# Strided sparse attention and a Mish MLP on one core: batch 0's strided keys over two DMA queues, and a new order of the steps in every block

## Chip, core and metric

The kernel runs on one core of a Trainium2 chip, in one launch. The metric is device time in microseconds (us). A core has five engines with their own instruction queues: PE (TensorE: matmuls, and transposes done as matmuls), ACT (ScalarE), DVE (VectorE), POOL (GpSimd) and SP (SyncE). DMAs are issued from SP, from ACT (both through the hardware queues) and from POOL (through the software queue). Here only POOL's loads change the type on the way, from float32 in device memory to bf16 in the core's memory. An engine executes its own instructions in order; engines wait for one another on semaphores.

## What is computed

Eight batches of attention with 8 heads over 576 tokens, head size 64. Heads 0 to 3 see the last 32 positions, heads 4 to 7 the positions with the same remainder modulo 32. The result, 4608 tokens by 512, goes through an MLP.

```python
mask_local = (rel >= 0) & (rel < 32)
mask_strided = (rel >= 0) & (pos[None, :] % 32 == pos[:, None] % 32)
attn = softmax(where(mask, q @ k.T / 8, -1e9)) @ v
x = attn.transpose(0, 2, 1, 3).reshape(4608, 512)
h = x @ w_in                       # 512 x 2048
g = h * tanh(log1p(exp(min(h, 20))))   # h itself above 20
out = g @ w_out                    # 2048 x 512
```

## The kernel before

**Attention.** A batch b is a class `Attn` with a strided half ("s", heads 4 to 7) and a local half ("l", heads 0 to 3), each cut in parts: s0, s1, s2 and l0, l1, l2. For batches 0 to 2 the loaded rows `ks`, `qs`, `kl`, `ql` are transposed on PE (step `T`, two halves each) into a PSUM bank and copied from there to `kTs`, `qTs`, `kTl`, `qTl` (step `t`, on ACT or DVE); from batch 3 on SP transposes them by DMA (step `D`). Then for each part: `q` (scores, PE), `e` (Exp, ACT), `k` (mask, DVE; in batch 0 a bias `b` added on PE takes its place), `v` (times v, PE), `r` (division by the sum, DVE). `sp` copies the strided v to the layout in use, `sh` copies the rows of the local v that two windows share. `X` and `Y` transpose the result on PE, with `xc` and `yc` as their copies to `xT`; later batches do it by DMA (`y`, `V`, `vc`). `xT` holds four batches, a ring.

**MLP.** It goes in 9 blocks of 512 tokens. Block 0 uses plain products (`p1`, `pm`, `p2`, `oc`) for half of its first layer and all of its second. Everything else uses a form with seven products on 2 x 2 sub-blocks instead of eight. A first-layer group g (four per block) has the PE steps `1:g` to `7:g`, four matmuls of 256 columns each, and between them the copies and sums `1c`, `5c` (ACT or DVE), `6c`, `7c` (DVE), then the Mish activations `E`, `H`, `Z` (ACT). `6` adds to the bank that `1c` has to have read; `7` and `3` follow `6c`; `4` follows `7c`. Two sets of three PSUM banks (SET/EE) alternate between groups. The second layer of block t-1 has the steps `m1` to `m7` (two halves of eight matmuls) and runs at the start of block t. Sums of weights (`sw` for w_in, `so` for w_out), of inputs (`x`) and of activations (`g`, `n`) are on DVE.

**Order.** Nothing is scheduled by a compiler. Strings of such words, run through `do` one by one, set the order on every engine at once: `IN` (block 0), `SECOND`, `THIRD`, `MAIN` (used for blocks 3 and 4), `M5`, `M6`, `P7`, `PLAIN`, `LAST`. `un` is a matmul whose result nobody reads; it stands only where PE waits for the first loads.

**Loads.** POOL issues all loads but one pair: `stage_ks` (L134) has SP load batch 0's strided k in float32, two heads at a time, into `hh[0]` and `hh[1]`, and `cast_ks` (L137) turns them into bf16 `ks`. Eight loads of the software queue can be under way; the ninth waits for the first to land. The weights come in four pieces each (`wi`, `wo`).

Line numbers: L121 is every matmul through `mm`, L201 and L207 the transposes of strided and local rows, L110 and L112 copies on ACT and DVE, L115 sums on DVE, L275 and L273 Exp, L318 and L320 the division, L306 times v, L350 `X`/`Y`, L684 `pm`, L444, L446 and L448 the Mish steps E, H and Z, L130, L132, L143, L150, L154, L156, L159, L172 and L175 the loads of POOL.

Of the kernel before, what the change touches and what calls it, by code (L numbers as in the profile page):

```python
# [19 lines left out]
SU = 80  # L20
# [25 lines left out]
def kernel(ctx, tc, q, k, v, moe_w_in, moe_w_out, out):  # L46
# [81 lines left out]
    def load_str(b, n, src):  # L128
        if b == 0:
            Po.dma_start(raw[n][0:SU], rows80(src, 4, 4))  # L130
        else:
            Po.dma_start(raw[n][0:PN], src[b, 4:8].rearrange("h (p j) d -> p h (j d)", j=CS))  # L132

    def stage_ks(hp):  # L134
        nc.sync.dma_start(hh[hp][0:SU], rows80(k, 4 + 2 * hp, 2))

    def cast_ks(hp, eng):  # L137
        cast(eng, ks[0:SU, 2 * hp:2 * hp + 2, :], hh[hp][0:SU])
# [32 lines left out]
    def load_w_in(f0, f1):  # L171
        Po.dma_start(w_in[:, :, f0:f1], moe_w_in.rearrange("(cc p) f -> p cc f", p=128)[:, :, f0:f1])  # L172
# [382 lines left out]
    with tc.manual_schedule():  # L555
        Sc.preload_act_table(AF.Exp)
        Sc.dma_start(consts[:], consts_h.ap())
        for hp in range(2):
            stage_ks(hp)
# [48 lines left out]
        def do(w, t):  # L608
            if w[0] == "^":
                w, t = w[1:], t + 1  # L610
# [16 lines left out]
            elif f == "kc":  # L627
                cast_ks(int(x[0]), eng)
            elif f == "wi":
                load_w_in(int(x[0]), int(x[1]))  # L630
# [84 lines left out]
        def go(plan, t=0):  # L715
# [3 lines left out]
        IN = (  # L719
# [23 lines left out]
        )  # L743
        SECOND = (
# [7 lines left out]
        )  # L752
        THIRD = (
# [10 lines left out]
        )  # L764
        MAIN = (
# [8 lines left out]
        )  # L774
        M5 = (
# [8 lines left out]
        )  # L784
        M6 = (
# [66 lines left out]
```

## Time and profile before

| | before |
|---|---|
| median of 3 runs | 286.04 us (285.47 to 286.15) |
| the profiled execution's own time | 286.13 us |
| its span, first to last instruction | 284.4 us |
| PE busy / weight loads (PEld) | 276.1 us (97%) / 226.4 us (80%) |
| DVE busy | 220.4 us (77%) |
| ACT busy | 193.1 us (68%) |
| POOL busy | 51.8 us (18%) |
| granted TensorE clock | 1.000 |
| chain that ended last | PE 90%, DMA 3%, ACT 3%, DVE 1%, issue 1% |

A row of the timeline gives start, length, engine, line, operation, what it writes and reads, the size, and how many are merged into the row; in brackets the idle time of the engine ahead of it and what ended it. A busy PE counts each matmul until its result is out, so two matmuls overlap, and a short pause between two does not show as idle: start-to-start times show it. The difference between the profiled time and the span, 286.13 - 284.4 = 1.7 us, lies around the first and the last instruction.

### The profile page before, as it was taken

To read this page: it belongs to the slowest core of one execution; us is meant where nothing else is said; L and a number is where in the kernel's file an instruction comes from. 1 tells how busy PE (TensorE), PEld (TensorE's weight loads), DVE (VectorE), ACT (ScalarE), POOL (GpSimd) and SP (SyncE) were. 2 spreads that over 40 slices of the span, in tenths; PEclk is the share of its full clock that TensorE was granted. 3 is DMA by queue.
4 is the path that set the end of the run, shared out by engine and by line. 5 is a ranking of instruction groups with operands and counts; after the bars stand their busy time and mean duration, and the time that the engine had idled before them with its cause. 6 is when DMAs were issued, how large, how long until landed. Compare 5 with 4: busy or idle time off the path is not lost.

```text
span 284.4 us, 7635 instructions
## 1 busy us (share of the span) xinstructions
PE 276.1 (97%) x3242; PEld 226.4 (80%) x3242; DVE 220.4 (77%) x376; ACT 193.1 (68%) x296; POOL 51.8 (18%) x65
## 2 busy tenths in 40 slices
PE   8889999999999999999999999999999999999994
PEld 2656845668988888988898888898888888888883
DVE  2588978899897897999798969885999656835753
ACT  2686884599867777669765986678879427525830
POOL 8423321350007005200350044002000000000000
PEclk9999999999999999999999999999999999999999
DMA  7999999999849988999799979998472030003003
GB/s 157 191 206 204 205 189 199 103 222 167 148 90 93 131 154 150 205 145 170 208 143 126 179 204 160 121 168 189 97 190 48 2 120 28 2 3 148 2 0 148
DMA packets 103826, 38.50 MB, mean 135 GB/s; under 512 B 85384, under 2 KB 99112, under 8 KB 103792
## 3 DMA queue, kind: packets, MB, share of 16 engines
q0 software_dynamic: 61296, 18.62, 66.7%
q1 hardware_dynamic: 42208, 19.14, 28.3%
q8 instruction: 25, 0.41, 0.6%
q10 hardware_dynamic: 288, 0.25, 0.4%
q14 instruction: 9, 0.07, 0.1%
HBM read 38.03 MB, written 9.44 MB: 167 GB/s over the span
## 4 chain that ended last, share of the span: by engine, by line
PE 90%; DMA 3%; ACT 3%; DVE 1%; issue 1%; POOL 0%; ACTq 0%; DVEq 0%; POOLq 0%
PE set L121 57%; PE ee L121 21%; PE at L306 5%; PE at L121 4%; DMA kl<-in_k_dram 3%; PE at L350 1%; PE ee L207 1%; PE ee L350 1%; ACT osb L110 1%; DVE ee L115 1%; PE set L306 0%; ACT kTl L110 0%; ACT gT L684 0%; ACT Ps L273 0%; DVE x_s L320 0%
## 5 line engine op out<-in xcount | busy, mean ns | idle before, releaser
L121 PEld LDWEIGHTS <-wis 128*128 128x128 bf16 x578 | 55.7, 98 | 11.6 <-issue 2.9
L121 PEld LDWEIGHTS <-gs 128*128 128x128 bf16 x512 | 48.9, 98 | 6.3
L121 PEld LDWEIGHTS <-gT 128*128 128x128 bf16 x448 | 42.1, 98 | 9.4
L121 PEld LDWEIGHTS <-w_in 128*128 128x128 bf16 x436 | 41.1, 97 | 8.1 <-issue 1.0
L121 PE MATMUL set<-xT,w_in 128*128 128x256 bf16 (+1 forms) x296 | 45.8, 278 | 0.4 <-ACT gT L684 0.2
L121 PE MATMUL set<-w_out,gT 128*128 128x256 bf16 (+1 forms) x304 | 46.2, 295 | 0.0
L448 ACT ACTIVATE gT<-set 128x1024 bf16<-128x1024 f32 x35 | 35.9, 1025 | 12.6 <-PE set L121 12.3
L121 PE MATMUL set<-xs,wis 128*128 128x256 bf16 x280 | 42.0, 272 | 0.3 <-DVE ee L115 0.2
L110 ACT COPY set<-set 128x512 f32<-128x512 f32 x37 | 21.4, 577 | 18.8 <-PE set L121 18.3
L115 DVE TENSOR_TENSOR hh<-set,hh 128x512 f32<-128x512 f32 x35 | 24.0, 686 | 7.2 <-PE set L121 6.9
L115 DVE TENSOR_TENSOR ee<-set,hh 128x512 f32<-128x512 f32 x35 | 24.4, 697 | 5.7 <-PE set L121 4.0
L121 PE MATMUL set<-wos,gs 128*128 128x256 bf16 x224 | 27.8, 273 | 0.0
L446 ACT ACTIVATE gT<-hh 128x512 bf16<-128x512 f32 x35 | 21.7, 633 | 1.8 <-DVE hh L115 1.6
L115 DVE TENSOR_TENSOR gs<-gT,gs 128x2048 bf16<-128x2048 bf16 x16 | 19.5, 1219 | 3.3 <-issue 1.0
L673 POOL COPY hold<-xT 1x2 bf16<-1x2 bf16 x6 | 2.3, 381 | 105.4 <-DMA xT<-x_l 105.4
L444 ACT ACTIVATE gT<-ee 128x512 bf16<-128x512 f32 x35 | 20.0, 596 | 2.0 <-PE ee L121 2.0
L121 PE MATMUL ee<-xs,wis 128*128 128x256 bf16 x140 | 21.0, 273 | 0.0
L121 PE MATMUL set<-xs,w_in 128*128 128x256 bf16 x140 | 21.0, 272 | 0.0
L121 PE MATMUL ee<-xT,wis 128*128 128x256 bf16 x140 | 21.0, 273 | 0.0
L115 DVE TENSOR_TENSOR gs<-gT 128x2048 bf16<-128x2048 bf16 x16 | 19.5, 1217 | 0.0
L320 DVE TENSOR_TENSOR x_s<-at,rden 72x768 bf16<-72x768 f32 (+1 forms) x22 | 18.8, 856 | 0.8
L121 PE MATMUL ee<-wos,gT 128*128 128x256 bf16 x128 | 16.1, 273 | 0.0
(135 smaller groups left out, 439.7 us busy)
## 6 DMA issues: line engine op xcount, KB each, us to landing
out_dram<-osb SPq DMA_DIRECT2D x17, 512.0 KB, 3.3
ql<-in_q_dram POOLq DMA_DIRECT2D x8, 288.0 KB, 11.9
vl<-in_v_dram POOLq DMA_DIRECT2D x8, 288.0 KB, 12.0
w_in<-in_moe_w_in_dram POOLq DMA_DIRECT2D x4, 512.0 KB, 15.0
w_out<-in_moe_w_out_dram POOLq DMA_DIRECT2D x4, 512.0 KB, 16.9
ks<-in_k_dram POOLq DMA_DIRECT2D x7, 288.0 KB, 11.2
qs<-in_q_dram POOLq DMA_DIRECT2D x7, 288.0 KB, 10.4
vraw<-in_v_dram POOLq DMA_DIRECT2D x7, 288.0 KB, 9.4
```

The costliest lines, as they stand in the source:

```text
L110: Sc.copy(out_, in_)
L115: eng.tensor_tensor(out=out_, in0=a, in1=b, op=op)
L121: PE.matmul(o, lhsT=lhsT, rhs=rhs, start=start, stop=stop, skip_group_check=True)
L207: PE.transpose(tr[64 * e:64 * e + 64, PL * j:PL * j + PL], src[0:PL, 2 * hp + e, j, :], ident[0:PL, 0:PL],)
L306: PE.matmul(po[:, (n - n0) // per, (n - n0) % per, :], lhsT=pt[0:r, c0:c0 + 128], rhs=rhs, start=True, stop=True,)
L320: Dv.tensor_tensor(out=xo, in0=po[0:m, :, :, 0:D], in1=rd.unsqueeze(3).to_broadcast([m, nb, per, D]), op=ALU.mult,)
L350: PE.transpose(tr[:, n * j:n * j + n], x[0:n, u:u + 2, :].rearrange("p u d -> p (u d)"), ident[0:n, 0:n],)
L444: Sc.activation(o[:, 0:2, 256:512], two(E), AF.Mish)
L446: Sc.activation(o[:, 2:4, 256:512], two(h[:, 1, :]), AF.Mish)
L448: Sc.activation(o[:, :, 0:256].rearrange("p (b u) n -> p b u n", b=2), SET[z][:, 0:2, :].rearrange("p b (u n) -> p b u n", u=2), AF.Mish,)
L673: Po.tensor_copy(hold[0:1, 0:2], src)
```

## The change

Batch 0's strided k: SP loads the first two heads (`stage_ks`, `hh[0]`) as before; the other two come through the software queue straight into `ks` as bf16, as POOL's first load (`load_str` with h = 2). One cast is left, on ACT. The first quarter of w_in is loaded in two halves of its rows. All words are put in a new order, and every block has its own string in `PLANS`; `_` before a word means the block before, as `^` means the next. Blocks 8 and 9 have the words that PLAIN and LAST had, in the same order. What is computed stays the same; six more `un` matmuls are issued in front.

```diff
     def load_str(b, n, src):
         if b == 0:
-            Po.dma_start(raw[n][0:SU], rows80(src, 4, 4))
+            h = 2 if n == "ks" else 0
+            Po.dma_start(raw[n][0:SU, h:4], rows80(src, 4 + h, 4 - h))
...
-    def stage_ks(hp):
-        nc.sync.dma_start(hh[hp][0:SU], rows80(k, 4 + 2 * hp, 2))
-
-    def cast_ks(hp, eng):
-        cast(eng, ks[0:SU, 2 * hp:2 * hp + 2, :], hh[hp][0:SU])
+    def stage_ks():
+        nc.sync.dma_start(hh[0][0:SU], rows80(k, 4, 2))
+
+    def cast_ks(eng):
+        cast(eng, ks[0:SU, 0:2, :], hh[0][0:SU])
...
-    def load_w_in(f0, f1):
-        Po.dma_start(w_in[:, :, f0:f1], moe_w_in.rearrange("(cc p) f -> p cc f", p=128)[:, :, f0:f1])
+    def load_w_in(f0, f1, c0=0, c1=4):
+        Po.dma_start(w_in[:, c0:c1, f0:f1], moe_w_in.rearrange("(cc p) f -> p cc f", p=128)[:, c0:c1, f0:f1])
...
-        for hp in range(2):
-            stage_ks(hp)
+        stage_ks()
...
-            if w[0] == "^":
-                w, t = w[1:], t + 1
+            while w[0] in "^_":
+                w, t = w[1:], t + (1 if w[0] == "^" else -1)
...
-        IN = (
-            "ld:qs@0 ld:vs@0 kc:0:D kc:1:A un:1:a un:1:a un:1:a un:1:a un:1:a un:1:a un:1:a un:1:a clear:1 clear:0 b:s1:C@0 "
...
+        PLANS = (
+            (
+                "un:1:a ld:ks@0 un:1:a kc:A un:1:a un:1:a un:1:a un:1:a un:1:a ld:qs@0 un:1:a ld:vs@0 un:1:a un:1:a "
...
-        go(LAST, NBLK)
+        for t, plan in enumerate(PLANS):
+            go(plan, t)
```

Three places show how instructions move.

POOL at the very start, its first loads; `ks`, `qs`, `vraw`, `kl`, `ql`, `vl_78` belong to batch 0. Before:

```order
L130 DMA qs<-in_q_dram 80x4x512
L154 DMA vraw<-in_v_dram 80x4x512
L143 DMA kl<-in_k_dram 96x4x384
L143 DMA ql<-in_q_dram 96x4x384
L159 DMA vl_78<-in_v_dram 96x24x64
L172 DMA w_in<-in_moe_w_in_dram 128x4x512 x3
```

Now:

```order
L131 DMA ks<-in_k_dram 80x2x512
L131 DMA qs<-in_q_dram 80x4x512
L155 DMA vraw<-in_v_dram 80x4x512
L144 DMA kl<-in_k_dram 96x4x384
L144 DMA ql<-in_q_dram 96x4x384
L160 DMA vl_78<-in_v_dram 96x24x64
L173 DMA w_in<-in_moe_w_in_dram 128x2x512 x2
```

Half of k stands in front of everything on the software queue; the rest keeps its order, and the first quarter of w_in is two loads.

ACT in batch 0's attention (`Ps` and `Pl` are the Exp results of the strided and local parts, `ee_103` and `ee_104` the banks of the transposes). Before:

```order
L110 CAST ks<-hh_69 80x1024
L110 COPY kTs<-ee_103 128x8x72
L110 COPY qTs<-ee_104 128x8x72
L275 ACTIVATE Ps_86<-at 72x2x288
L275 ACTIVATE Ps_85<-set_102 72x2x432
L275 ACTIVATE Ps_84<-set_101 72x2x432
L110 COPY kTl<-ee_104 128x576
L110 COPY qTl<-ee_104 128x576
L110 COPY qTl<-ee_103 128x576
L275 ACTIVATE Pl_89<-at 128x2x384
```

Now:

```order
L110 CAST ks<-hh_68 80x1024
L110 COPY kTs<-ee_104 128x8x72
L110 COPY qTs<-ee_103 128x8x72
L110 COPY qTs<-ee_104 128x8x72
L276 ACTIVATE Ps_86<-at 72x2x288
L276 ACTIVATE Ps_85<-set_102 72x2x432
L276 ACTIVATE Ps_84<-set_101 72x2x432
L110 COPY kTl<-ee_103 128x576
L110 COPY qTl<-ee_104 128x576
L110 COPY qTl<-ee_103 128x576
L276 ACTIVATE Pl_89<-at 128x2x384
```

Both copies of the transposed q are now on ACT, ahead of the first Exp; DVE had one of them. On PE the transposes of `ql` moved ahead of two of the three `v` steps.

DVE where block 0 ends and block 1 begins (`wos` are the sums of w_out, `xs` those of the inputs, the copies those of batch 2's transposes, `set_101<-set_101` is `1c:0` of block 1). Before:

```order
L112 COPY kTs<-ee_104 128x8x72
L115 TENSOR_TENSOR xs<-xT 128x512
L115 TENSOR_TENSOR wos<-w_out 128x2048
L115 TENSOR_TENSOR wos<-wos,w_out 128x2048
L115 TENSOR_TENSOR wos<-w_out,wos 128x2048
L112 COPY qTl<-ee_104 128x576
L115 TENSOR_TENSOR xs<-xT,xs 128x512
L112 COPY qTl<-ee_103 128x576
L112 COPY vs<-vraw 72x32x64
L112 COPY vl_78<-vl_78 32x4x5x64
L112 COPY set_101<-set_101 128x512
```

Now:

```order
L115 TENSOR_TENSOR wos<-w_out 128x2048
L115 TENSOR_TENSOR xs<-xT 128x512
L112 COPY kTs<-ee_104 128x8x72
L115 TENSOR_TENSOR wos<-wos,w_out 128x2048
L115 TENSOR_TENSOR xs<-xT 128x512
L112 COPY qTs<-ee_103 128x8x72
L115 TENSOR_TENSOR wos<-w_out,wos 128x2048
L112 COPY kTl<-ee_103 128x576
L112 COPY qTl<-ee_104 128x576
L115 TENSOR_TENSOR xs<-xT,xs 128x512
L112 COPY qTl<-ee_103 128x576
L112 COPY set_101<-set_101 128x512
```

The big sums stand further ahead and apart from one another, one copy of `qTs` and one of `kTl` came over from ACT, and the two copies of v went behind `1c:0`.

More of the change, by code (lines that the diff above doesn't have):

```diff
@@ L627, in do @@
             elif f == "kc":
-                cast_ks(int(x[0]), eng)
+                cast_ks(eng)
             elif f == "wi":
-                load_w_in(int(x[0]), int(x[1]))
+                load_w_in(*(int(c) for c in x))
             elif f == "wo":
@@ L717, in go @@
                 do(w, t)
-        IN = (
[23 rows of a table removed]
-        )
-        SECOND = (
[7 rows of a table removed]
-        )
-        THIRD = (
[10 rows of a table removed]
-        )
-        MAIN = (
[8 rows of a table removed]
-        )
-        M5 = (
[8 rows of a table removed]
-        )
-        M6 = (
[7 rows of a table removed]
-        )
-        P7 = (
[5 rows of a table removed]
-        )
-        PLAIN = (
[4 rows of a table removed]
-        )
-        LAST = (
-            "m1c:D g:1 m5:0 m5:1 m5c:A g:2 m6:0 m6:1 g:3 m2:0 m6c:A m2:1 m7:0 m7:1 m7c z:b:D w:b:S m3:0 m3:1 m3c "
-            "st:1 m4:0 m4:1 z:1:A z:0:D w:0:S w:1:A "
-        )
-        go(IN)
-        go(SECOND, 1)
-        go(THIRD, 2)
-        for t in range(3, NBLK):
-            main = {5: M5, 6: M6}.get(t, MAIN)
-            if t + 1 < B:
-                go(" ".join(w for w in main.format(n1=t + 2, n2=t + 3).split() if int(w.partition("@")[2] or 0) < B), t)
-            else:
-                go(P7 if t + 1 == B else PLAIN, t)
-        go(LAST, NBLK)
+        PLANS = (
+            (
[23 rows of a table added]
+            ),
+            (
[7 rows of a table added]
+            ),
+            (
[10 rows of a table added]
+            ),
+            (
[8 rows of a table added]
+            ),
+            (
[8 rows of a table added]
+            ),
+            (
[8 rows of a table added]
+            ),
+            (
[7 rows of a table added]
+            ),
+            (
[5 rows of a table added]
+            ),
+            (
[4 rows of a table added]
+            ),
+            (
+                "m1c:D g:1 m5:0 m5:1 m5c:A g:2 m6:0 m6:1 g:3 m2:0 m6c:A m2:1 m7:0 m7:1 m7c z:b:D w:b:S m3:0 m3:1 m3c "
+                "st:1 m4:0 m4:1 z:1:A z:0:D w:0:S w:1:A "
+            ),
+        )
+        for t, plan in enumerate(PLANS):
+            go(plan, t)
 _INS = ['q', 'k', 'v', 'moe_w_in', 'moe_w_out']
```

150 rows, old and new, of tables (IN, M5, M6, MAIN) are left out of this document.

## The prediction

> **What bounds the kernel now.** I read the page first, then a table of stages, then the timeline in the stages where the table shows idle time. On the page PE has little left, and its clock is at full speed throughout:
>
> ```profile
> PE 276.1 (97%) x3242; PEld 226.4 (80%) x3242; DVE 220.4 (77%) x376; ACT 193.1 (68%) x296; POOL 51.8 (18%) x65
> PEclk9999999999999999999999999999999999999999
> ```
>
> The stages are cut where PE's work changes: waiting for k and q, batch 0's attention, the start of the MLP, block 0's rest, the hand-over to block 1, blocks 1 to 6, block 7, block 8 with the tail.
>
> ```profile
> core 0: us, PE busy (x) PEld busy (x) DVE busy (x) ACT busy (x) POOL busy (x), PEclk, DMA share, GB/s
> 0.00:8.60 8.60, 6.60 (x33) 2.34 (x33) 2.59 (x17) 2.86 (x3) 6.44 (x12) 1.00 0.86 166
> 8.60:19.30 10.70, 9.59 (x211) 6.70 (x211) 6.99 (x15) 8.18 (x14) 4.35 (x6) 1.00 1.47 197
> 19.30:28.00 8.70, 8.11 (x68) 5.22 (x66) 7.65 (x18) 5.59 (x8) 2.85 (x4) 1.00 1.25 204
> 28.00:57.00 29.00, 28.97 (x386) 18.27 (x384) 24.28 (x45) 19.94 (x32) 8.59 (x11) 1.00 1.33 174
> 57.00:64.00 7.00, 6.42 (x109) 4.74 (x109) 6.94 (x13) 7.00 (x14) 3.43 (x4) 1.00 1.63 223
> 64.00:225.00 161.00, 160.91 (x1950) 140.84 (x1949) 138.02 (x227) 122.52 (x188) 26.13 (x30) 1.00 1.12 145
> 225.00:256.00 31.00, 31.00 (x281) 27.18 (x279) 18.63 (x27) 14.52 (x23) 0.00 (x0) 1.00 0.09 36
> ```
>
> PE idles 0.59 us in 19.3 to 28, 0.58 us in 57 to 64, and 0.09 us in the 161 us after that. So a new order can win in the first 64 us, and by short pauses that busy time hides; in the 161 us it can only keep or lose. The first MLP product starts near 19.3; all before it is worth what batch 0's attention waits.
>
> **Part 1, the head (0 to 23.5).** These rows carry it:
>
> ```profile
> 0.74 0.90 SPq L135 DMA_DIRECT2D hh<-in_k_dram  x2
> 1.29 0.76 POOL L130 DMA_DIRECT2D qs<-in_q_dram  x1 [0.84 <-POOLq L836]
> 4.00:6.00 2.00, 2.00 (x7) 0.59 (x6) 0.54 (x1) 0.00 (x0) 2.00 (x4) 1.00 1.08 212
> hh<-in_k_dram SPq DMA_DIRECT2D x2, 320.0 KB, 5.1
> 8.64 0.57 PEld L201 LDWEIGHTS <-qs 72*128 72x128 bf16 x16 [0.41 <-DMA qs<-in_q_dram]
> 9.19 0.46 DVE L112 COPY qTs<-ee 128x576 bf16<-128x576 bf16 x1 [0.40 <-PE ee L201]
> 9.38 0.64 ACT L110 COPY qTs<-ee 128x576 bf16<-128x576 bf16 x1 [1.03 <-PE ee L201]
> 10.57 0.65 ACT L275 ACTIVATE Ps<-at 72x576 bf16<-72x576 f32 x1 [0.56 <-PE at L121]
> 11.54 0.45 PE L207 MATMUL ee<-consts_sb,kl 96*64 96x96 bf16 x12 [0.19 <-DMA kl<-in_k_dram]
> 14.23 1.18 ACT L110 COPY qTl<-ee 128x576 bf16<-128x576 bf16 x2 [0.85 <-PE ee L207]
> 17.00 0.87 ACT L273 ACTIVATE Pl<-ee 128x384 bf16<-128x384 f32 x2
> 19.20 0.95 DVE L320 TENSOR_TENSOR x_l<-at,rden 96x768 bf16<-96x768 f32 x1
> 20.44 0.41 DVE L115 TENSOR_TENSOR xs<-xT 128x512 bf16<-128x512 bf16 x1
> ```
>
> q's landing at 8.64 starts the chain. The GB/s count what is written. The change takes one 320 KB load off SP and puts 160 KB (80 x 1024 bf16) ahead of q on POOL's queue: 160 KB less in front of q, at 212 GB/s up to 0.77 us earlier. But q is issued one POOL instruction (0.76 us) later; if that is what starts its transfer, it lands up to 0.76 later. Between these ends I take -0.4, nearer the gain: q takes 7.3 us from issue to landing, far more than its issue, so it mostly queues for bandwidth.
>
> From landing to the first Exp it takes 10.57 - 8.64 = 1.93 us, with the two copies of q side by side. Now both are on ACT, one behind the other: the first at about 8.64 + 0.55 = 9.19, ends of 9.83 and 10.47 against 10.02 now, +0.45. Then ACT runs from 10.57 to 17.87 (17.00 + 0.87), and 0.85 us of that is idle ahead of the `ql` copies, since PE does all of v first. With the `ql` transposes ahead of two of the v steps most of it closes: -0.6, with 0 and -0.85 as bounds. Behind it on DVE come the divisions, and now a sum of x and one of w_in (0.41 each) ahead of the last copy to `xT`; the four matmuls that need no such copy cover most of it, +0.15. Of the cast that is gone (1.0 us, DVE) nothing counts: DVE waits there anyway. The local k (11.54, 0.19 idle) moves with q. Sum -0.4; ends -0.77 - 0.85 + 0.45 = -1.2 and 0.76 + 0.45 + 0.15 = +1.4. The split of w_in's first quarter costs one POOL issue behind all of batch 0's loads: nothing, as long as w_in is waited for nowhere. It landed by 17.95, ahead of 19.3:
>
> ```profile
> 17.95 0.76 POOL L175 DMA_DIRECT2D w_out<-in_moe_w_out_dram  x1 [1.95 <-DMA w_in<-in_moe_w_in_dram]
> ```
>
> The Trainium skill, "DMA: Bandwidth & Descriptors", section "Issuing engines are not separate DMA queues", says that DMAs from different engines run on the same 16 DMA engines and interleave, and that issuing from several saves only issue time. By that rule the split moves no landing, the head comes to +0.0 in place of -0.4, and the sum below to 285.5; no row here shows the two halves apart.
>
> **Part 2, the start of the MLP (19.3 to 28).**
>
> ```profile
> 23.48 0.60 PE L121 MATMUL set<-xT,w_in 128*128 128x256 bf16 x4 [0.25 <-ACT gT L684]
> 24.01 0.60 PE L121 MATMUL ee<-xs,wis 128*128 128x256 bf16 x4
> 24.17 0.57 ACT L110 COPY set<-set 128x512 f32<-128x512 f32 x1 [0.21 <-PE set L121]
> 24.79 0.60 PE L121 MATMUL set<-xT,w_in 128*128 128x256 bf16 x4 [0.18 <-ACT set L110]
> 26.09 0.42 PE L201 MATMUL at<-consts_sb,ks 72*128 72x72 bf16 x8
> 26.68 0.60 PE L121 MATMUL set<-xs,wis 128*128 128x256 bf16 x4 [0.16 <-DVE ee L115]
> 28.89 1.02 ACT L448 ACTIVATE gT<-set 128x1024 bf16<-128x1024 f32 x1
> ```
>
> A step of four matmuls takes 0.44 us start to start where nothing waits (256.26 to 256.69 in a row further down). `1:1` starts at 23.48, `5:1` at 24.01, `2:1` at 24.79: 0.34 us lost to `1c`. Ahead of `7:1` (26.68) eight transposes of about 0.31 us started at 26.09: 0.28 lost to `6c`. The first wait (Mish of block 0's bank) stays. Now `5:1` and `5:2` stand behind `1:1`, and both pairs of eight transposes ahead of `7:1`, so -0.62 at best. But `5:2` needs a DVE sum of w_in two places earlier than before, and the next user of the bank waits for the Mish step at 28.89 (1.02 us) as it does now, which may give it all back: 0 at worst. I take -0.35.
>
> **Part 3, the hand-over (57 to 64).** ACT is busy 7.00 of 7.00 and DVE 6.94. One copy of `qTs` and one of `kTl` (0.6 each) go from ACT to DVE ahead of this stage, and the three 1.22 us sums of w_out start earlier. What stays is the row of Exp steps, each of which frees a bank for the next scores and then for `1:1`:
>
> ```profile
> 58.29 0.92 ACT L275 ACTIVATE Ps<-at 72x864 bf16<-72x864 f32 x1
> 60.09 0.20 PE L121 MATMUL ee<-qTl,kTl 64*128 64x96 bf16 x1 [0.22 <-ACT Ps L273]
> ```
>
> The first Exp still stands behind the copy of block 0's output (`oc:0`), so I give it -0.15, between -0.58 (all idle gone) and +0.6 (one more Exp in front of `1c:1`).
>
> **Part 4, blocks 1 to 6.** `6` may start 0.87 us after the end of `1` (23.48 + 0.44 = 23.92 to 24.79) if ACT takes `1c` at once. The new strings put just two steps (0.88 us) between them in eleven groups, where the old ones had three or more; in return `7` now stands three steps behind `6`, not two. Where ACT happens to be inside another step, the wait is half of 0.57 to 1.02, some 0.4 us. For two such groups in eleven that is +0.8; for none 0, for six +2.4. The longer `6` to `7` brings back some 0.1 us each in three groups. I take +0.2, nearer to none since PE idles 0.09 us in all of the stage today with steps as tight as that.
>
> **Part 5, block 7.** Pauses that busy time hides, the first and the last of the stage:
>
> ```profile
> 232.52 0.60 PE L121 MATMUL ee<-xs,wis 128*128 128x256 bf16 x4
> 233.04 0.60 PE L121 MATMUL set<-xs,wis 128*128 128x256 bf16 x4
> 239.96 0.60 PE L121 MATMUL set<-xT,w_in 128*128 128x256 bf16 x4
> 240.39 0.60 PE L121 MATMUL set<-xs,wis 128*128 128x256 bf16 x4
> 240.97 0.60 PE L121 MATMUL set<-xs,w_in 128*128 128x256 bf16 x4
> 256.26 0.60 PE L121 MATMUL set<-xT,w_in 128*128 128x256 bf16 x4
> 256.69 0.60 PE L121 MATMUL set<-xs,wis 128*128 128x256 bf16 x4
> ```
>
> 239.96 to 240.39 is a step without a wait (0.43), 240.39 to 240.97 one with 0.14 behind it: two steps do not cover a 0.69 us sum on DVE with its hand-overs. The block has seven such places, from 0.08 (232.52 to 233.04) to 0.14; the new string has three steps in most. -0.3, between -0.6 and 0. Blocks 8 and 9 keep their order: 0.
>
> **Sum.** -0.4 - 0.35 - 0.15 + 0.2 - 0.3 = -1.0. Against the profiled execution's own 286.13 (span 284.4 and 1.7 around it) that is 285.1; the median of the runs, 286.04, lies 0.09 lower, so it is a gain of 0.33%. About 0.3% (0.86 us, 285.18) is what a measurement of this kernel can tell from no change. The likeliest case's own range is 284.3 to 286.0.
>
> **Rivals.** A, slower: ACT does not take `1c` at once in blocks 1 to 6. Six of eleven groups at 0.4 us are +2.4 in place of +0.2, so 287.3; it decides from about four groups on. For it: DVE is busy 138 of 161 us and ACT 122.5, so queues are rarely empty. Against: these engines run in order and the old strings leave 0.09 us idle at the same load. B, larger gain: q lands 0.77 earlier, and the moved sums free the hand-over of its whole 0.58 us: -0.8, -0.6 and -0.55 for parts 1 to 3 with 0 and -0.3 for 4 and 5: 283.9. For it, DVE full in 57 to 64; against, ACT full there too. C, no change: the software queue starts q one issue later, +0.7 in the head instead of -0.4, the rest as above: 286.2. For it the row at 1.29, where q is POOL's first load today.
>
> **How the numbers follow.** Forecast 0.50, A 0.27, B 0.12, C 0.11. Faster by over 0.3%: half of the forecast's case, a little over (0.28), all of B (0.12), some of the rest (0.03): 0.43. Within 0.3% (285.18 to 286.90): 0.20 of the forecast's, 0.08 of C, 0.01 of A: 0.29. Slower: 0.28. The range that leaves out 2 in 10 is 283.9 to 287.6: B's time at the low end, A with one group more at the high end.
>
> **What would show it.** Head: `qs` awaited near 8.2 (C: 9.3), no idle of ACT ahead of the `qTl` copies, `1:1` starting by 23.1. Start of the MLP: `2:1` and `7:1` without a wait. Hand-over: PE's idle at or below 0.5 us between the `ql` transposes and `6:1` of block 1. Blocks 1 to 6: PE idle below 0.5 us with no row of `6` behind an ACT copy; A is right if that idle exceeds 2 us. Wrong altogether: a DVE or PE step that waits for a load of batch 3 or later, which no part counts.

## The result: slower, and the profile after

| | before | changed |
|---|---|---|
| median | 286.04 us (285.47 to 286.15) | 302.85 us (4 runs, 299.72 to 308.04) |
| the profiled execution: time / span | 286.13 / 284.4 us | 308.04 / 306.2 us |
| ratio to the kernel before | | 1.055, 95% interval 1.047 to 1.064 |

The change costs some 16 us, far outside the predicted range. All ratios here leave out executions more than 1.5% longer than the shortest one of the same kernel, so a ratio can differ from that of two medians, and the profile after is of such an execution, the longest of its four. The first lines of the page after:

```profile
PE 281.7 (92%) x3248; PEld 228.6 (75%) x3248; DVE 220.3 (72%) x377; ACT 193.4 (63%) x294; POOL 51.7 (17%) x67
PEclk9999999999999999999989999999999997999999
PE 65%; DMA 10%; DVE 8%; issue 2%; ACT 1%; POOL 0%; DVEq 0%; ACTq 0%; POOLq 0%; SPq 0%
```

DVE and ACT are busy as long as before (220.4 and 193.1 us), so no work was added. PE fell from 97% to 92% of a longer span: it waits. On the chain that ended last its share fell from 90% to 65%, DMA rose from 3% to 10% and DVE from 1% to 8%. The stages of the prediction, now cut where about as many matmuls have been done (columns as there; the first two stages in one up to 19.3, the next two up to 58.8):

```profile
0.00:19.30 19.30, 16.94 (x250) 9.72 (x251) 8.28 (x29) 11.10 (x17) 11.99 (x20) 1.00 1.18 176
19.30:58.80 39.50, 35.85 (x445) 23.25 (x442) 30.79 (x61) 26.69 (x41) 11.08 (x14) 1.00 1.32 175
58.80:65.60 6.80, 6.43 (x117) 4.34 (x111) 6.42 (x11) 5.62 (x12) 3.08 (x3) 1.00 0.99 161
65.60:242.00 176.40, 164.41 (x1950) 141.53 (x1948) 138.85 (x228) 123.08 (x187) 25.52 (x31) 0.99 1.25 134
242.00:277.10 35.10, 32.89 (x281) 28.01 (x279) 20.68 (x31) 14.00 (x21) 0.00 (x0) 0.95 0.08 32
277.10:306.20 29.10, 25.17 (x227) 21.77 (x224) 15.27 (x20) 12.91 (x20) 0.00 (x0) 0.99 0.19 73
```

Against 19.3, 37.7, 7.0, 161.0, 31.0 and 28.4 us before: 0, +1.8, -0.2, +15.4, +4.1 and +0.7, together 21.8 us, more than the 16 since this execution is the longest. Blocks 1 to 6, where the prediction allowed 0.2 us, lose most. What PE waits for, by groups (engine, tile and line, what it waited for: us in all, times, longest):

```profile
PE set L121 <- DVE ee L115: 6.0, 12, 1.3
PE set L121 <- DVE osb L115: 2.4, 4, 0.8
PE at L307 <- DMA vl<-in_v_dram: 2.3, 1, 2.3
PE at L351 <- DVE xT L112: 1.6, 1, 1.6
PE at L208 <- DVE kTl L112: 1.2, 1, 1.2
```

None of these groups stands among the first six of before, where the largest of them measures:

```profile
PE set L121 <- DVE ee L115: 0.2, 1, 0.2
```

Line numbers from L129 on are one higher than before. Three places show three kinds of wait. The first, from the timeline of PE and DVE in block 2 (`6:1`, `2:0`, `4:0`, `2:1` and `7:1` on PE, the sum `6c:1` on DVE):

```profile
97.88 0.60 PE L121 MATMUL set<-xs,wis 128*128 128x256 bf16 x4
98.31 0.60 PE L121 MATMUL set<-xT,w_in 128*128 128x256 bf16 x4
98.75 0.60 PE L121 MATMUL set<-xs,w_in 128*128 128x256 bf16 x4
99.19 0.60 PE L121 MATMUL set<-xT,w_in 128*128 128x256 bf16 x4
...
99.89 0.70 DVE L115 TENSOR_TENSOR ee<-set,hh 128x512 f32<-128x512 f32 x1 [1.33 <-PE set L121]
...
100.65 0.60 PE L121 MATMUL set<-xs,wis 128*128 128x256 bf16 x4 [0.86 <-DVE ee L115]
```

`6:1` has ended by 98.48, and `6c:1` reads what it wrote; yet DVE, idle for 1.33 us, begins at 99.89, 0.1 us behind the end of `2:1` (99.79). `2:1` writes the other bank of the set. Then `7:1` waits for `6c:1`. The second kind, from the timeline of PE and ACT in block 1 (`X:0`, `X:1` and the copy `xc:0`):

```profile
73.21 0.42 PE L351 MATMUL at<-consts_sb,x_s 72*128 72x72 bf16 x8
...
73.94 0.65 ACT L110 COPY xT<-at 128x576 bf16<-128x576 bf16 x1
...
74.64 0.42 PE L351 MATMUL at<-consts_sb,x_s 72*128 72x72 bf16 x8 [1.01 <-ACT xT L110]
```

`X:1` writes a bank of its own, and still begins only when `xc:0` has read the other one (73.94 + 0.65 = 74.59). The third, the longest stall, from the timelines of POOL, PE and ACT:

```profile
145.02 2.40 POOL L160 DMA_DIRECT2D vl<-in_v_dram  x2
...
155.13 0.60 PE L121 MATMUL set<-xT,w_in 128*128 128x256 bf16 x4
158.06 0.22 PE L307 MATMUL at<-vl,Pl 128*128 128x65 bf16 x2 [2.33 <-DMA vl<-in_v_dram]
159.35 0.71 PE L307 MATMUL at<-vl,Pl 128*128 128x65 bf16 x10 [1.07 <-ACT vl L110]
159.87 1.90 PE L121 MATMUL set<-w_out,gs 128*128 128x256 bf16 x8
```

The local v of batch 5 lands 13 us after its issue. Behind the stall eight matmuls take 1.69 us from start to start (161.56 - 159.87 by the next row) where eight took 0.87.

The transposes that SP issues by DMA land later as well; issue to landing from 64 to 200 us, the kernel before first:

```profile
xT<-x_l SPq DMA_TRANSPOSE x10, 3.0
kTl<-kl SPq DMA_TRANSPOSE x5, 4.2
```

And the changed kernel:

```profile
xT<-x_l SPq DMA_TRANSPOSE x9, 7.2
kTl<-kl SPq DMA_TRANSPOSE x5, 9.7
```

So two theories. **Whole tiles**: the waits are kept per PSUM tile, not per bank. `SET[i]` and `AT` are each one tile of two banks, so two steps on different banks wait for each other, and which one waits is set by which is written first in the strings. The semaphore waits of the built programs, resolved to the steps, bear it out: in the kernel before no `2` waits for a `6c` and no `6c` for a `2`, since every `2` is written ahead of its `6`. The new strings put `2` behind `6` in 28 groups, and

```
14 groups: 6c:g waits for the last matmul of 2:g     (block 2: 6c:1 <- PE 2:1)
11 groups: 2:g waits for the sum 6c:g or 7c:g        (block 0: 2:2 <- DVE 6c:2)
 3 groups: neither
```

**Collision**: POOL's small copies (`hold`), by which the kernel before keeps the next loads back until the transposes of x have landed, wait for an older batch in the new strings and hold no load back: four of the six that run find their batch landed, and the two that wait, until 205.94 and 230.98 us, stand behind the last load (189.13). Loads and transposes then run together and both come late. The rivals kept from the prediction: ACT late for `1c` (no such wait is among the groups above), and the loads of batch 0.

### The profile page after: what moved, and what is told of

Read it like the earlier page. It is cut to its first block, busy times and chain, and to the rows that moved or that the text cites. A ratio compares the mean times of both kernels' runs of the same rounds, so it can differ in the third digit from the quotient of the medians.

```text
span 306.2 us, 7657 instructions
## 1 busy us (share of the span) xinstructions
PE 281.7 (92%) x3248; PEld 228.6 (75%) x3248; DVE 220.3 (72%) x377; ACT 193.4 (63%) x294; POOL 51.7 (17%) x67
## 4 chain that ended last, share of the span: by engine, by line
PE 65%; DMA 10%; DVE 8%; issue 2%; ACT 1%; POOL 0%; DVEq 0%; ACTq 0%; POOLq 0%; SPq 0%
PE set L121 41%; PE ee L121 15%; DMA vl<-in_v_dram 4%; PE at L307 3%; DMA kTs<-ks 3%; PE at L121 3%; DVE ee L115 3%; DMA xT<-x_l 3%; DVE gs L115 1%; DVE hh L115 1%; DVE osb L115 1%; PE ee L208 1%; DVE vl L112 0%; ACT vl L110 0%; PE at L351 0%
## 5 line engine op out<-in xcount | busy, mean ns | idle before, releaser
L121 PEld LDWEIGHTS <-wis 128*128 128x128 bf16 x584 | 56.9, 99 | 16.3 <-issue 6.5
L110 ACT COPY set<-set 128x512 f32<-128x512 f32 x33 | 18.9, 574 | 22.4 <-PE set L121 22.3
L110 ACT COPY osb<-set 128x1024 f32<-128x1024 f32 x9 | 9.1, 1013 | 12.3 <-PE set L121 12.3
L110 ACT COPY hh<-ee 128x512 f32<-128x512 f32 x22 | 12.9, 591 | 6.2 <-PE ee L121 6.2
```

What stands on the lines that cost most here:

```text
L110: Sc.copy(out_, in_)
L121: PE.matmul(o, lhsT=lhsT, rhs=rhs, start=start, stop=stop, skip_group_check=True)
```

## Experiments

Each ratio is to the kernel before, run beside it on the same chip. The changed kernel's is 1.055 (1.047 to 1.064); in us, a ratio is taken times 286.

**Step 2 ahead of 6 again (two_ahead).** In 28 groups, for instance in block 2:

```diff
- 5:1 E:0 6:1 5c:1:A 7c:0 k:s1:D@3 2:0 4:0 2:1 6c:1
+ 5:1 E:0 2:1 6:1 5c:1:A 7c:0 k:s1:D@3 4:0 6c:1
```

> The changed kernel with each step 2 of a first-layer group put back just ahead of step 6 of its group (28 groups of blocks 0 to 7); nothing else. Theory, whole tiles: SET is one tile of two banks, so 2 (which adds to the first bank) and the sum 6c (which reads the second) wait for each other although they share no byte; with 2 ahead of 6 no such wait is left. The 6.0 us in which PE waits for the sum 6c fall below 2, and the time falls by 4 to 8 us, to 294 to 299. Rival, ACT late for 1c: step 2 itself needs 1c, so the time stays within 1 us of the changed kernel's 302.9. Rival, late loads: within 1 us too.

297.31 us, ratio 1.041 (1.035 to 1.047). The group of the 6.0 us:

```profile
PE set L121 <- DVE ee L115: 1.7, 6, 0.4
```

As expected: some 4 us of the 16 (1.4%, between 0.3 and 2.5 by the two intervals) come back with nothing but the place of `2`. ACT's rival falls, since `2` too needs `1c`.

**The mirror: step 2 behind 6c in the kernel before (two_behind).** 16 words of the strings for blocks 3 to 7, for instance

```diff
- 2:2 6:2 ld:qs@{n2} 1:3 1c:3:A 6c:2 v:s2:A
+ 6:2 ld:qs@{n2} 1:3 1c:3:A 6c:2 2:2 v:s2:A
```

> The kernel before with one kind of step moved in blocks 3 to 6 (and block 7): each step 2 of a first-layer group from ahead of 6 to just behind the sum 6c in the strings, 16 moves over one to three places; its own input (1c) is long done there. Theory, whole tiles: 2 now waits for 6c, 0.5 to 2 us a group, and the time rises by 10 to 22 us, to 296 to 308. If banks counted singly: 2 waits for nothing and the time stays within 1 us of 286.2.

303.59 us, ratio 1.062 (1.059 to 1.065; two runs), with the head, the loads and all other words as before. The group that has 0.2 us in the kernel before is now the first:

```profile
PE set L121 <- DVE ee L115: 12.4, 14, 1.7
```

This step alone can cost what the whole change cost.

**Only the text (at_text).** Three copies of `AT` written one place later; for instance

```diff
- X:0:a xc:0:a:A ld:kl@3 X:1:A
+ X:0:a ld:kl@3 X:1:A xc:0:a:A
```

> The changed kernel with three copies written one place later in the strings (xc:0 behind X:1 in blocks 1 and 2, the second copy of batch 1's local k behind the transposes into the other bank). Every engine keeps exactly its order; only which of two steps on different banks of AT comes first in the program changes, and so which one waits. Theory, whole tiles: the stalls of 1.1 us at 73, 1.8 us at 110 and 1.2 us at 37 shrink, together by 2 to 4 us; the time falls to 299 to 301. Any theory that counts by banks or by the order on the engines: no change, within 0.5 us.

301.01 us, ratio 1.047 (1.044 to 1.050). No engine's order changes, and PE's wait of 1.01 us is gone, and with it the groups of 1.6 and 1.2 us in the list above (0.6 us for `qTs` stands in place of the last). The two transposes are one row, from the timeline of PE:

```profile
71.97 0.68 PE L351 MATMUL at<-consts_sb,x_s 72*128 72x72 bf16 x16
```

The interval still overlaps the changed kernel's, and the profiled execution (305.33 us) has other long waits for DVE, so the row carries this more than the time: a wait that comes and goes with the text, on two banks of one tile, is what whole tiles predict and a count by banks or engines excludes.

**Both edits (two_and_text).** 

> The changed kernel with both edits of the first runs: step 2 ahead of 6 in 28 groups, and the three copies of AT's banks written one place later. If both act on waits of their own, the gains add: 302.9 - 5.5 - 1.8 = 295.5, between 294 and 297. If the first stall only hands over to the next: no lower than 297.

297.54 us, ratio 1.041 (1.038 to 1.043). The gains don't add: nothing below the first edit alone. The timelines of SP, DVE and PE say where it went:

```profile
108.08 1.97 SPq L328 DMA_TRANSPOSE xT<-x_l  x1
...
116.64 0.42 DVE L115 TENSOR_TENSOR xs<-xT 128x512 bf16<-128x512 bf16 x1 [6.08 <-issue]
...
117.45 0.68 DVE L112 COPY o<-set 128x512 f32<-128x512 f32 x1
...
118.19 1.22 PE L121 MATMUL set<-wos,gs 128*128 128x256 bf16 x5 [3.85 <-DVE o L112]
```

DVE stood for 6.08 us ahead of a sum of x (`x:2` of block 3) that the built program lets wait for the two transposes of batch 3, and the copy `o`, which PE needs, stood behind it. Transposes land late here too:

```profile
xT<-x_l SPq DMA_TRANSPOSE x10, 6.9
kTl<-kl SPq DMA_TRANSPOSE x5, 12.6
```

**One load earlier (vl_early).**

```diff
- Z:0 _hold@2 H:0
+ Z:0 ld:vl@5 _hold@2 H:0
- m6:1 _ld:vl@5 e:s0:F
+ m6:1 e:s0:F
```

> The changed kernel with one load moved: the local v of batch 5 is issued in block 3, ahead of the wait of POOL for block 2's transposes, not in block 4 behind three other loads. Theory, late loads: the wait of 4.9 us of ACT and 2.3 us of PE for this load goes, and with it PE's 4.5 us of idle from 155 to 160, so the time falls by 3 to 6 us, to 297 to 300. Whole tiles alone: no change, within 1 us of 302.9.

302.85 us, ratio 1.056 (1.052 to 1.060): a miss. In the profiled execution (307.98 us) the wait for the local v is gone, and PE stands some 15 us earlier instead, behind DVE, which waits for the strided v:

```profile
142.40 0.69 DVE L112 COPY vs<-vraw 72x2048 bf16<-72x2048 bf16 x1 [4.37 <-DMA vraw<-in_v_dram]
...
143.75 1.01 PE L121 MATMUL set<-xT,w_in 128*128 128x256 bf16 x4 [4.32 <-DVE ee L115]
```

The stall is not tied to that one load: here another late load takes its place.

**No holding back, in the kernel before (no_hold).** The five `hold` words left out (six copies, since MAIN runs twice).

> The kernel before without the five small copies by which POOL waits for the transposes of x before it issues the next batch's loads; nothing else. Theory, transposes and loads collide: in the changed kernel these copies wait for an older batch and hold nothing back, the transposes of kTl take 9.7 us to land in place of 4.2 and those of xT 7.2 in place of 3.0. Without them the kernel before shows the same: xT above 4.5 us, and 0.5 to 4 us lost. Rival, the order of the strings alone: no change, within 0.5 us.

289.9 us median (10 runs, 285.94 to 292.68), ratio 1.007 (1.004 to 1.011). POOL in the kernel before, at the copy that waits for batch 2:

```profile
84.93 0.63 POOL L673 COPY hold<-xT 1x2 bf16<-1x2 bf16 x1 [23.04 <-DMA xT<-x_l]
```

POOL and PE in this run, profiled in an execution of 292.64 us:

```profile
79.34 0.71 POOL L132 DMA_DIRECT2D ks<-in_k_dram  x1 [17.73 <-DMA kTs<-ks]
...
92.87 1.04 PE L121 MATMUL set<-xT,w_in 128*128 128x256 bf16 x4 [3.91 <-DMA xT<-x_l]
```

Without it the loads of batch 4 start at 79.34, before that copy has even run, and PE then waits 3.91 us for transposes of x. These take 4.4 us in the middle, where above 4.5 was expected; the ratio is as expected, some 2 us. A wait of 3.91 us belongs to this long execution and not to the 2 us; no profile of a shorter one was taken. That the copies are worth something in the old order is shown, that the collision is what they prevent there is read off this one profile.

**Holding back, in the changed kernel (hold_back, hold_and_vl).** On top of both edits, the loads of batches 4 to 7 behind the transposes of x of two batches earlier. For batch 6 (of the strings, only the words that issue DMAs or run on POOL):

```diff
- y:1 _y:0 ld:vs@6 _ld:qs@6 _ld:ks@6 _ld:vl@5 ld:vl@6
+ y:1 _y:0 hold@4 ld:vs@6 _ld:qs@6 _ld:ks@6 _ld:vl@5 ld:vl@6
```

In the second run `ld:vl@5` also moved out of there to block 3, behind `ld:vs@5`.

> The run before with POOL's waits put back: the loads of batches 4, 5, 6 and 7 behind the transposes of x of batches 2, 3, 4 and 5, as the kernel before has them. Theory, collision: xT lands in 3 to 4.5 us, the stalls where DVE waits for xT near 91 and 150 shrink, 1 to 3 us below the run before. Rival: later loads make a wait of their own for k, q or v of batches 6 and 7, and the time rises.

> The run hold_back with one more edit: the local v of batch 5 issued in block 3, ahead of POOL's new wait for the transposes of batch 4, so that this load is not held back with the others. Theory, collision of loads and transposes: with the loads of the next batch kept off the transposes, and no load late for that, the one long stall of PE (3.6 to 4.4 us with the slower matmuls behind it) goes for good: 4 to 8 us below hold_back's 301.7 and 3 to 6 us below two_and_text's 297.5, to 291 to 295. Rival: the stall comes back at another load, and the time stays at 297 or above.

301.68 and 301.57 us, ratios 1.054 (1.048 to 1.060) and 1.055 (1.049 to 1.060): both slower than without, so the time follows the rival both times. xT lands in 3.2 us in both, as the theory has it, but other transfers are late in turn, and not the ones that the rivals named: in the first the local v of batch 5 (PE's waits),

```profile
PE at L307 <- DMA vl<-in_v_dram: 4.0, 1, 4.0
```

in the second the transposes of the strided x in block 6 (timeline of DVE):

```profile
205.18 1.34 DVE L112 COPY xT<-ks 128x576 bf16<-128x576 bf16 x2 [3.77 <-DMA ks<-x_s]
```

PE waits 4.2 us behind that copy. In the new strings, putting the old holds back moves the long stall on in both.

**A quarter of the bytes (light_two_and_text, light_after, light_load_alone).** Every instruction stays where it is; for instance in `load_str`:

```diff
+ n_h = 4 if b < 4 else 1
- ... src[b, 4:8] ...
+ ... src[b, 4:4 + n_h] ...
```

> The run two_and_text with the loads of batches 4 to 7 cut to one head of four (a quarter of the bytes; the other three heads then hold what an earlier batch left, so that part of the result is not computed). All instructions of all engines stay in number and order. Theory, collision: the loads no longer slow the transposes of xT, kTl and qTs, the one long stall (3.9 us with 2.4 us of slow matmuls behind it) is gone in every run: 289 to 292. Rival, the order of the strings on DVE is what stalls: 296 or more.

> The changed kernel with the loads of batches 4 to 7 cut to one head of four, in the same way. Theory: of the 302.9 us the part of the whole-tile waits stays and the part of the collisions goes: 302.9 less 5 to 8, so 295 to 298, and the spread of the runs (299.7 to 308.0) shrinks below 2 us. Rival: 301 or more.

> Control: the run load_alone with the same cut of the loads of batches 4 to 7. Theory: that order keeps loads and transposes apart already, so the time falls by no more than 1 us from 285.75.

292.14 us, ratio 1.021 (1.019 to 1.023), so 5.7 us (2.0%) less than with all bytes; 299.82, ratio 1.048 (1.045 to 1.051); and the control 285.12, ratio 0.997 (0.996 to 0.999), like load_alone below. In the first of the three:

```profile
xT<-x_l SPq DMA_TRANSPOSE x10, 3.1
kTl<-kl SPq DMA_TRANSPOSE x5, 4.8
```

This settles the collision where the tile waits are gone: with the same order on every engine and the bytes of four batches cut, xT lands in 3.1 us in place of 6.9 and the long stall is gone. The cut also makes the loads themselves land sooner (the local v in 3.0 us in place of 10.9); how much of the 5.7 us that is worth was not separated. In the changed kernel itself the same cut brings 2 us by the ratios, less than the 5 to 8 expected, and no more than that kernel's own interval; its spread shrinks from 8.3 to 2.0 us, as expected. So the two causes overlap: taking the tile waits away is worth 4 us with all bytes (1.055 to 1.041) and 7.8 with a quarter of them (1.048 to 1.021). That one wait covers another is the likely reason; no run shows it directly.

**The loads alone (load_alone).** The kernel before with `stage_ks`, `cast_ks` and `load_str` as changed, and these words:

```diff
- ld:qs@0 ld:vs@0 kc:0:D kc:1:A
+ ld:ks@0 ld:qs@0 ld:vs@0 kc:A
- wi:0:512
+ wi:0:512:0:2 wi:0:512:2:4
```

> The kernel before with the change of the loads alone: half of batch 0's strided k by the software queue as its first load, one cast, w_in's first quarter in two parts; all strings as before but for these words. If the loads explain the loss, 290 or more. Theory: 286.1 within 0.7, since the first wait moved by 0.35 us only.

285.75 us (10 runs), ratio 0.998 (0.997 to 0.999): 0.7 us faster, between 0.3 and 1.0. Of the versions that compute everything it is the only one that beats the kernel before.

**The first two blocks alone (head_new_rest_old).** Strings of blocks 0 and 1 from the run with both edits, then the old ones.

> Blocks 0 and 1 in the changed kernel's order, with step 2 ahead of 6 and the copies of AT's banks behind both transposes, and with the change of the loads; from block 2 on the strings of the kernel before. PE's pauses before 80 us add up to 6.7 us in two_and_text and to 8.4 in load_alone, and from 80 us on to 2.6 in load_alone. Theory, the new order of the first two blocks is worth what the prediction gave it once its waits are gone: 284 to 285.5, a gain of 0.2 to 0.7% over the kernel before. Rival, the gain is the loads' alone: 285.7 or more.

287.2 us, ratio 1.005 (1.003 to 1.006): 2 us slower than the loads alone. Even with `2` ahead of `6` and the copies of `AT`'s banks moved, the new order of the first blocks loses. Its longest groups of waits, the head aside:

```profile
PE set L121 <- DVE ee L115: 1.3, 4, 0.4
PE ee L121 <- DVE osb L115: 1.2, 1, 1.2
```

The second stands in block 3 (at 123.74 us), outside the new strings, and load_alone has one of 0.6 us for `osb` too; which of the two comes of the new order was not tested.

**One more try at a gain (load_and_hold).** On load_alone, `hold@3` moved ahead of `ld:ql@5` and `ld:kl@5`.

> The run load_alone with POOL's wait for the transposes of batch 3 put ahead of the loads of batch 5's local q and k, not behind them. There DVE waits for these transposes until 113.3 us and PE pauses 0.72 us behind it. Theory, collision: the transposes land earlier and the pause goes, 0.3 to 0.8 us below load_alone, 285.0 to 285.5. Rival: the transposes are late for another reason, no change within 0.3 us of 285.75.

285.76 us (12 runs, 284.76 to 287.26), ratio 1.000 (0.998 to 1.001). PE's pause (0.6 us for `osb` by load_alone's list of waits) is gone from the profile, but no gain over load_alone (0.998) shows: a miss. The 0.3 to 0.8 us below load_alone that were expected would be a ratio of 0.995 to 0.997, outside the interval.

## Why the prediction was wrong

The step that failed is Part 4, "`6` may start 0.87 us after the end of `1`", and the count that follows it. It priced a new string by two distances, from `1` to `6` and from `6` to `7`, and did not mention the place of `2`, which counts it as free: `2` writes one bank and `6c` reads the other. In 25 of the 28 groups the built program has a wait between the two. (The eleven groups are counted rightly; that `7` stands three steps behind `6` in return holds for four of them.) The term of +0.2 measured +15.4 in the profiled execution, and Part 5, reckoned in the same way at -0.3, measured +4.1. The place of `2` is not all of that: over the whole kernel the tile waits are worth 4 to 8 us. The other large cost shown, up to 5.7 us, is one that no part had a term for: transfers of later batches that land late.

| what | from ratio to ratio | us |
|---|---|---|
| waits on whole tiles (both edits) | 1.055 to 1.041 | 4.2 |
| bytes of the loads of batches 4 to 7 | 1.041 to 1.021 | 5.7 |
| order of blocks 0 and 1 | 1.005 to 0.998 | 2 |
| left, in blocks 2 to 8: cause open | | 4.6 |
| the loads of batch 0 | 0.998 | -0.7 |

The rows hold for this order of taking away: with the loads' bytes cut first (1.055 to 1.048), they are worth 2 us and the tile waits 7.8. The 4.6 is what remains of 1.021 - 0.998 = 2.3% (6.6 us) after the 2 us of blocks 0 and 1. The profile of light_two_and_text suggests short waits for sums and copies on DVE (the longest behind the head is 0.8 us, for `osb`); no run took it apart. The first row carries the changed kernel's own interval, 2.5 us either way.

- **Part 1, the head.** The term of the loads was -0.4 and measured -0.7 (-0.3 to -1.0) for the whole kernel; q is awaited until 8.29, not 8.64, as said, and rival C (9.3) is out. By the rule of the Trainium skill, "DMA: Bandwidth & Descriptors", section "Issuing engines are not separate DMA queues", this term was 0; the interval leaves it out, if narrowly, but load_alone also writes 160 KB less and has a cast less, and no run tells these from the second queue. The other half of that rule, that DMAs of all engines interleave on the same 16 DMA engines, agrees with the collision: 6.9 against 3.1 us for xT. The new order of the head gained nothing that shows: `1:1` starts between 22.90 and 23.91 in the ten profiles that have it, between 22.64 and 23.48 in the three with the old head and between 22.60 and 23.07 in the three with the loads alone. Profiles of one head differ by 0.5 to 1 us, more than the whole term of -0.4, so the 8.29 of one profile proves little.
- **Part 2, the start of the MLP.** -0.35 predicted, `2:1` and `7:1` without a wait. `2:1` has none, but `7:1` waits 0.32 us and `2:2` 1.27 us for the sum `6c`. Rows 19.3 to 58.8 lost 1.8 us.
- **Part 3, the hand-over.** -0.15 predicted, -0.2 measured. One profile of each can't tell that from chance, so the mechanism (copies to DVE) is not shown.
- **Rival A** had the right sign and the wrong cause: PE does not wait for `1c` on ACT in any group of the list above, it waits for sums on DVE.
- **The last clause** came true: PE and DVE waited for loads and transposes of batches 3 and later, which no part counted. The prediction followed POOL's order in the head only, and did not look at which batch each `hold` waits for.

## What to carry to other kernels

Before a step is moved, read from the built program what each instruction waits for, not from which bytes it touches. Where one tile spans two banks, steps on either bank can wait for one another, and the order in the text decides which one waits. A delay on a DMA queue that looks like idle time may be what keeps two kinds of transfers apart; ask what it waits for before it is moved. When a stall moves as soon as its transfer is made early, measure the bytes by cutting them, not the next transfer in line.

## What the runs showed of the hardware

Two short pauses of PE close together were followed by matmuls at half speed. In block 7 of the changed kernel, by start times, with the row of 254.2 to 257.5 last (columns as in the stages, the granted clock 0.51):

```profile
252.21 1.03 PE L121 MATMUL set<-xs,wis 128*128 128x256 bf16 x8 [0.86 <-DVE ee L115]
254.19 1.01 PE L121 MATMUL set<-xT,w_in 128*128 128x256 bf16 x4 [0.95 <-DVE ee L115]
254.99 1.06 PE L121 MATMUL set<-xs,w_in 128*128 128x256 bf16 x4
255.85 1.06 PE L121 MATMUL ee<-xT,wis 128*128 128x256 bf16 x4
...
257.55 0.65 PE L121 MATMUL ee<-xT,wis 128*128 128x256 bf16 x4
...
254.20:257.50 3.30, 3.30 (x16) 2.36 (x16) 0.00 (x0) 1.41 (x2) 0.00 (x0) 0.51 0.00 0
```

After two waits of 0.86 and 0.95 us a step takes 0.85 us (255.85 - 254.99) in place of 0.44, until 257.55, 3.4 us after the second wait; the mean granted clock of 242.0 to 277.1 is 0.95. The four steps add 1.6 us to two waits of 1.8. A single pause did not do this: behind the 1.01 us ahead of 74.64 a step takes 0.44 us (74.89 to 75.33 by the next rows) and the granted clock is 1.00 from 74 to 77, and in two_behind 14 waits of up to 1.7 us leave it at 1.00 from 64 to 260. The Trainium skill, "TensorE: Matmul & The Clock Gate", section "Part 1: The HAM clock gate (the \"warmup\" mystery)", states half the clock after at least one idle window of about 3.4 us, and full speed again after a busy one. The 3.4 us of slow steps agree; that the whole window has to be idle does not, since PE worked between the two waits.
